# One stream of attention pairs: who empties v's product, when row sums are inverted, and who cuts the diagonal blocks

## The chip, the cores and the metric

One NeuronCore of one Trainium2 chip runs the whole program. The metric is the time of one execution in microseconds (us) on the device; lower is better. The kernel before takes 553.42 us, the median of three runs (552.69 to 554.0).

## The reference, cut to what matters

Attention over 4 batches of 8 heads with 576 positions and 64 dimensions in a head, then two layers on its output:

```
q_rot, k_rot = rotate(q), rotate(k)
scores = q_rot @ k_rot.T / sqrt(64)
scores = scores - max(scores, axis=-1)
attn = exp(scores); attn = attn / (sum(attn, axis=-1) + 1e-9)
x = (attn @ v), heads side by side                # (4, 576, 512)
h = gelu(x @ w_in); u, v = halves of h            # w_in, w_out, ... are float64
gated = u * (w_sg @ layer_norm(v) + b_sg)
x = x + gated @ w_out
out = (sigmoid(causal_conv(x)) * (x @ w_val)) @ w_out2
```

Only the attention is touched by the change. Its products must hold float32 precision: q and k are split into a high and a low part (tiles QH, QL, KH, KL), and three products of them are added.

## The kernel before, in words

The 32 heads are worked off as 16 **pairs** (pair 0 to 15), two heads on the upper and the lower 64 partitions. In `phase(i)` TensorE computes the exponents of pair i and, between them, the scores of pair i+1 that are needed only for their row maximum. The order of these units is written out by hand in `ORDERS` (line 25): a letter for the unit and a digit for the PSUM slot (`PS[0]` to `PS[3]`, two banks each). The letters are:

- `t`: one of eight units of the transposed scores of pair i (`st_unit`, line 663): three split products and the product that subtracts the row maximum, 8 matmuls. ScalarE takes the exponential out of PSUM into a tile `e` (line 674).
- `T`: the same for the last 64 keys of both heads (line 671). It reads KRH and KRL, k's last 64 columns laid out as diagonal blocks of a 128x128 tile.
- `y` and `x`: scores of pair i+1 for the maximum (`s_unit`, line 612): 2 matmuls of 320 columns or 4 of 256. VectorE reduces them with a maximum (line 615).
- `S`: the same for the last 64 queries (line 622). It reads QR, q's last 64 columns as diagonal blocks; VectorE reduces it at line 624.

Below, a unit is named by its letter and its place in the order: y0, t1, y2, t3, t4, x5, t6, t7, t8, y9, t10, t11, y12, x13, T14, S15 for pairs 1 to 14. With the digits 0123012301230120 the slot of y0 is used again by t4 (and by t8, y12 and S15), that of x5 by y9 and x13.

After the phase come the product with v (`pv_unit`, line 698, then line 708), which always accumulates in slot 3, and the row sums (`sum_unit`, lines 732 and 735) in slot 2, with 24 matmuls at line 732 in pairs 1 to 8 and 16 in pairs 9 to 14, where GpSimd adds up more of the exponentials beforehand (`FOUR = 9`). The next pair's y0 follows at once. Slot 3 is then next written by t3, slot 2 by y2. Slot 3 is emptied by two copies into the tile XU, ScalarE for one head (line 712; in the profile L264, the helper's line) and VectorE for the other (line 713). The sums go through ScalarE (line 738) and a transposing transfer into RC (line 742); `sum_end` joins the two halves and inverts them on VectorE (lines 747 and 749: 128x9 elements) and stores them (line 753).

Between the last maximum and the next y0, VectorE rotates q and k of pair i+2 (`prep_high`, line 565 and 566, L260 in the profile), ScalarE rounds them (QP, QH, KH by L264), and in pairs 1 to 8 VectorE also converts a piece of a float64 weight (`wa_half`, lines 311 to 317). At the end of `prep_high` two transfers cut KRH out of KH (line 569, issued on SyncE by line 455) and ScalarE cuts QR out of the rotated q with two 64x64 copies (lines 573 to 576).

The order inside every engine but TensorE is set by a planner, `Plan`. Each piece of work is added with an engine, a cost, and keys that it reads and writes; `after` names more pieces that must be done first. The planner lets each engine take, of what is ready by its clock, the piece with the earliest due time. TensorE keeps the order of the program:

```
        if eng == "PE":
            if self.last_pe is not None:
                deps.add(self.last_pe)
            self.last_pe = k
```

So each queue is in order on the chip, and an instruction that waits holds up what stands behind it. `sum_end(i - 1)` is called behind the phase of pair i: in pairs 1 to 8 once S15 is reduced, in pairs 9 to 14 once the low part of k is made.

Of the kernel before, what the change touches and what calls it, by code (L numbers as in the profile page):

```python
# [21 lines left out]
B, HP, S, DM, HALF = 4, 4, 576, 512, 288  # L22
NPAIR = B * HP
FOUR = 9
ORDERS = ('xtttyttytyttyxTS', '0123012301230120'), ('ytyttxtttyttyxTS', '0123012301230120'), ('ttttttttT', '012012012')
UNITS = ((0, 0), (1, 0), (0, 1), (1, 1), (2, 0), (2, 1), (3, 0), (3, 1))


# [143 lines left out]
def mixer_kernel(ctx: ExitStack, tc: tile.TileContext, qk, v, cs, w_in, g_ln, w_sgT, b_sg,  # L172
# [387 lines left out]
    def prep_high(i, after):  # L560

        j2, j3 = i % 2, i % 3
        for j in (0, 1):
            raw, kr = RAW[j2][:, j], ("raw", j2, j)
            tt("D", lambda raw=raw: raw, lambda raw=raw: raw, lambda: cst, ALU.mult, 2 * S, [("cst",)], [kr], after)
            after = [tt("D", lambda raw=raw: raw[:, 0], lambda raw=raw: raw[:, 0], lambda raw=raw: raw[:, 1], ALU.add, S, [], [kr])]
            if j:
                acopy(lambda: KH[j3], lambda raw=raw: raw[:, 0], S, [kr], [("kh", j3)])
                dma(32, lambda q: dg(q, KRH[j3], KH[j3]), [("kh", j3)], [("krh", j3)], n=2)
            else:  # L570
                acopy(lambda: QP[j2], lambda raw=raw: raw[:, 0, 0:512].rearrange("r (p c) -> r c p", c=4), 1100, [kr], [("qp", j2)])
                acopy(lambda: QH[j3], lambda raw=raw: raw[:, 0], S, [kr], [("qh", j3)])
        for h in range(2):
            rows = slice(64 * h, 64 * h + 64)
            acopy(lambda rows=rows: QR[j3][rows, rows], lambda rows=rows: RAW[j2][rows, 0, 0, 512:S], 64, [("raw", j2, 0)], [("qr", j3)],
                  P.writer["kh", j3])
        return after

    def low_part(e, i, j, after):
# [108 lines left out]
    def pv_unit(i, us):  # L688
# [21 lines left out]
        add("PE", FP32 + 0.1, mm, [("e", EU[i, 8]), ("vm", j2)], [kp])  # L710
        xu = XU[j2]
        acopy(lambda: xu[:, 0], lambda: pv[:, 0, 0:HALF], HALF, [kp], [("xu", j2, 0)])
        add("DVE", dve(HALF), lambda: nc.vector.tensor_copy(xu[:, 1], pv[:, 1, 0:HALF]), [kp], [("xu", j2, 1)])

        def st(q):
            for hf in range(2):
# [55 lines left out]
    def attention():  # L772
# [3 lines left out]
        def phase(i, vl):  # L776

            nt, xs, ys = 0, iter(range(2)), iter(range(2, 6))
            for x, (what, k) in enumerate(zip(*ORDERS[(1 if i + 1 < NPAIR else 2) if i else 0])):
                k = int(k)  # L780
                if what in "tT":
                    u = 8 if what == "T" else nt
                    st_unit(i, u, PS[k], ("ps", k))
                    add_unit(i, u)
                    nt += what == "t"
                else:
                    s_unit(i + 1, {"x": xs, "y": ys, "S": iter((8,))}[what].__next__(), PS[k], ("ps", k))
                if not x:
                    first = [P.last_pe, *vl]
                    if 2 <= i + 1 < NPAIR:  # L790
                        prep_low(i + 1, first)
                if x == (12 if i < FOUR else 0):
                    job_s(i, [P.last_pe])
            if i + 1 < NPAIR:
                s_end(i + 1)

        vl = []
        for i in range(NPAIR):
# [6 lines left out]
            phase(i, vl)  # L805
            ep.append(P.last_pe)
            rot = [P.last_pe]
            if 0 < i < FOUR or i == NPAIR - 1:
                sum_end(i - 1, [*rot, *P.writer.get(("mn", (i + 1) % 2, 1), ())] if i + 1 < NPAIR else ())
            if i + 2 < NPAIR:  # L810
                rot = prep_high(i + 2, [P.last_pe, *P.writer[("mn", (i + 1) % 2, 1)]])
            vl = job_v(i, [P.last_pe], rot)
            if FOUR <= i < NPAIR - 1:
                sum_end(i - 1, P.writer["kl", (i + 1) % 3])
            for us in ((0, 2), (1, 3), (4, 5), (6, 7)):
                pv_unit(i, us)
            sum_unit(i, PS[2], ("ps", 2))
# [417 lines left out]
```

## Time and profile before

| what | value |
|---|---|
| median of three runs | 553.42 us (552.69 to 554.0) |
| the profiled execution, its own time | 551.67 us |
| its span, first to last instruction | 549.9 us |
| granted TensorE clock, whole span | 1.00 of full speed |
| TensorE / VectorE / ScalarE / GpSimd busy | 98% / 76% / 52% / 45% |
| attention | from the start to about 235 us |

The rest of the program, from about 235 us on, is the two layers (line 835). A timeline row gives start, duration, engine, line, operation, tiles written and read, shape, count, and in brackets how long the engine was idle before it and what ended that. Matmuls overlap, so the difference of two starts tells more than a duration; a matmul row that is longer than its neighbours of the same shape has waited. The engines' busy shares are averages over stages with different limits.

### The profile page before, as it was taken

The numbers are of one execution on the slowest core, as the hardware profiler recorded it, in microseconds if no ns is written. First come the engines' busy times: TensorE is split into PE (matmuls) and PEld (weight loads), VectorE is DVE, ScalarE is ACT, GpSimd is POOL, SyncE is SP. The second block draws the span as 40 slices with busy tenths as digits, with TensorE's granted clock in tenths as the row PEclk, the third lists the DMA queues.
The fourth block names the chain that finished last, engine by engine and source line by source line (L and its number), as shares of the span: only waits on it lengthen the run. The fifth ranks groups of instructions, "written<-read, shape, count | busy, mean of one in ns | idle before, by whom it ended". The sixth has DMA issues, their size and how long they took to land.

```text
span 549.9 us, 12860 instructions
## 1 busy us (share of the span) xinstructions
PE 540.3 (98%) x5104; PEld 463.2 (84%) x5104; DVE 416.2 (76%) x627; ACT 283.4 (52%) x479; POOL 246.0 (45%) x231
## 2 busy tenths in 40 slices
PE   7999999999999999999999999999999999999996
PEld 6877777777777777679989989989999998899985
DVE  7888888888888888869478945653989997659610
ACT  3577777777766667635426236134157443333311
POOL 6545555555555555446886676653610011221000
PEclk9999999999999999999999999999999999999999
DMA  5465655565665564674384662634364112110022
GB/s 191 137 195 139 178 155 170 152 184 159 202 162 165 154 203 96 185 248 116 125 277 145 207 214 73 212 106 147 108 213 130 65 44 77 39 58 2 0 77 95
DMA packets 55404, 77.07 MB, mean 140 GB/s; under 512 B 26768, under 2 KB 31376, under 8 KB 55344
## 3 DMA queue, kind: packets, MB, share of 16 engines
q1 hardware_dynamic: 55040, 75.98, 45.2%
q8 instruction: 40, 0.66, 0.5%
q10 hardware_dynamic: 304, 0.26, 0.1%
q14 instruction: 20, 0.16, 0.1%
HBM read 55.94 MB, written 18.95 MB: 136 GB/s over the span
## 4 chain that ended last, share of the span: by engine, by line
PE 80%; DVE 11%; DMA 3%; ACT 2%; issue 2%; SPq 0%; POOL 0%; DVEq 0%; ACTq 0%; POOLq 0%
PE psa L835 52%; PE psa L663 11%; PE psa L698 7%; DVE raw L260 5%; PE psa L612 3%; DVE mx L615 3%; PE psa L732 2%; PE psa L671 2%; ACT e L674 2%; PE psa L946 2%; DMA rr<-r_d 2%; PE psa L708 1%; DMA xs<-xu_d 1%; DMA raw<-qk 1%; ACT kh L264 1%
## 5 line engine op out<-in xcount | busy, mean ns | idle before, releaser
L615 DVE TENSOR_REDUCE mx<-psa 128x2 f32<-128x640 f32 (+1 forms) x96 | 88.7, 954 | 21.6 <-PE psa L612 14.3
L674 ACT ACTIVATE e<-psa 128x576 f32<-128x576 f32 x144 | 88.4, 652 | 17.8 <-PE psa L671 9.1
L698 PE MATMUL psa<-e,vm 128*32 128x288 f32 x1024 | 65.4, 408 | 0.0
L698 PEld LDWEIGHTS psa<-e,vm 128*32 128x32 f32 x1024 | 31.6, 110 | 27.8 <-issue 2.6
L261 POOL TENSOR_TENSOR ac<-e,e 128x576 f32<-128x576 f32 x32 | 45.4, 1435 | 8.1 <-ACT e L674 8.0
L835 PE MATMUL psa<-s_h,vn 128*128 128x288 f32 x256 | 46.8, 295 | 0.0
L264 ACT CAST qp<-raw 128x512 fp32r<-128x512 f32 x16 | 19.1, 1195 | 45.7 <-DVE raw L260 39.4
L260 DVE TENSOR_TENSOR raw<-raw,cst 128x1152 f32<-128x1152 f32 (+1 forms) x33 | 42.2, 1278 | 0.2 <-DMA raw<-qk 0.2
L663 PE MATMUL psa<-qh,kh 64*128 64x288 f32 x256 | 41.9, 309 | 0.0
L663 PE MATMUL psa<-qh,kl 64*128 64x288 f32 x256 | 40.0, 296 | 0.0
L663 PE MATMUL psa<-ql,kh 64*128 64x288 f32 x256 | 39.0, 291 | 0.0
L663 PE MATMUL psa<-mr,one_r 64*128 64x288 f32 x256 | 39.0, 291 | 0.0
L835 PEld LDWEIGHTS psa<-s_h,vn 128*128 128x128 f32 x256 | 38.3, 188 | 0.0
L261 POOL TENSOR_TENSOR vs<-vs,u 128x576 f32<-128x576 f32 x16 | 26.7, 1666 | 20.5 <-DVE vs L950 20.5
L612 PE MATMUL psa<-kh,qp 64*128 64x320 f32 (+1 forms) x256 | 32.9, 313 | 1.8 <-ACT kh L264 1.7
L1027 DVE SCALAR_TENSOR_TENSOR gt<-xm,cw,gt 128x576 f32<-128x576 f32 x32 | 29.0, 910 | 1.8 <-ACT gt L1024 1.4
L612 PEld LDWEIGHTS psa<-kh,qp 64*128 64x128 f32 x256 | 21.6, 184 | 9.5 <-ACT kh L264 7.2
L663 PEld LDWEIGHTS psa<-qh,kh 64*128 64x128 f32 x256 | 25.8, 184 | 3.3 <-DVE mx L615 1.5
L835 PE MATMUL psa<-XH,w_l 128*128 128x288 f32 x128 | 27.4, 296 | 0.1
L835 PE MATMUL psa<-XL,w_h 128*128 128x288 f32 x128 | 27.3, 295 | 0.0
L835 PE MATMUL psa<-XH,w_h 128*128 128x288 f32 x128 | 27.3, 295 | 0.0
L835 PE MATMUL psa<-s_l,vn 128*128 128x288 f32 x128 | 27.3, 294 | 0.0
(185 smaller groups left out, 1474.3 us busy)
## 6 DMA issues: line engine op xcount, KB each, us to landing
raw<-qk SPq DMA_DIRECT2D x31, 576.0 KB
vm<-v SPq DMA_DIRECT2D x16, 288.0 KB
xu_d<-xu SPq DMA_DIRECT2D x32, 144.0 KB
rb<-r_d SPq DMA_DIRECT2D x32, 144.0 KB
xs<-xu_d SPq DMA_DIRECT2D x16, 288.0 KB
x_d<-xs SPq DMA_DIRECT2D x16, 288.0 KB
g_d<-vs SPq DMA_DIRECT2D x16, 288.0 KB
wr<-w_in SPq DMA_DIRECT2D x8, 512.0 KB
```

The costliest lines, as they stand in the source:

```text
L260: return add("DVE", dve(n), lambda: nc.vector.tensor_tensor(out_(), a(), b(), op), r, w, after, lock=True)
L261: return add("Pool", pool(n), lambda: nc.gpsimd.tensor_tensor(out_(), a(), b(), op), r, w, after, lock=True)
L264: return add("Act", act(n), lambda: nc.scalar.copy(out_(), in_()), r, w, after)
L612: nc.tensor.matmul(ps[:, h, w * y:w * y + w], QP[j2][rows, c], kh[rows, keys], start=True, stop=True)
L615: add("DVE", MAXIMA[n // 2 > 0][1], lambda: nc.vector.tensor_reduce(out=MX[j2][:, n // 2 > 0, :, chunks[0]:chunks[-1] + 1], in_=ps[:, :, 0 ...
L663: nc.tensor.matmul(ps[:, h, 0:HALF], x[rows, keys] if o < 3 else x[rows], y[rows, cols], start=o == 0, stop=o == 3)
L671: nc.tensor.matmul(ps[:, hf, 0:HALF], x, y[:, cols], start=o == 0, stop=o == 3)
L674: add("Act", 0.62, lambda: nc.scalar.activation(E[n], ps[:, :, 0:HALF], AF.Exp), [kps], [("e", n)])
L698: nc.tensor.matmul(pv[32 * t:32 * t + 32, h, 0:HALF], VM[j2][:, 128 * j + 64 * h + 32 * (t % 2):128 * j + 64 * h + 32 * (t % 2) + 32], E[E ...
L732: nc.tensor.matmul(ps[32 * t:32 * t + 32, 0, 0:HALF], ones[h], a[:, h], start=n == 0, stop=False, skip_group_check=True)
L835: nc.tensor.matmul(out_(y), lhs(p, k, y), rhs(q, k, y), start=not z, stop=ends and z == len(terms) - 1)
L1027: add("DVE", dve(S) + 0.05, lambda dd=dd, m=m, x2=x2, gt=gt: nc.vector.scalar_tensor_tensor(gt(), x2()[:, m:m + S], cw[:, 5 * dd + m:5 * d ...
```

## The change

Four edits, all in the attention. (1) For pairs 0 to 8 ScalarE makes both copies out of v's product; from pair 9 on VectorE keeps one. (2) `sum_end(i - 1)` is called inside the phase of pair i, behind the unit at place 8, for all pairs 1 to 15. (3) KRH is cut by two ScalarE copies behind the phase of the pair before, and QR by two transfers behind QH; before, it was the other way round. (4) Pairs 9 to 14 have an order of their own, in which the third y moves from place 12 to place 8: y0, t1, y2, t3, t4, x5, t6, t7, y8, y9, t10, t11, t12, x13, T14, S15, over the same slots.

```diff
-ORDERS = ('xtttyttytyttyxTS', '0123012301230120'), ('ytyttxtttyttyxTS', '0123012301230120'), ('ttttttttT', '012012012')
+ORDERS = ('xtttyttytyttyxTS', '0123012301230120'), ('ytyttxtttyttyxTS', '0123012301230120'), ('ttttttttT', '012012012'), ('ytyttxttyytttxTS', '0123012301230120')
...
             if j:
                 acopy(lambda: KH[j3], lambda raw=raw: raw[:, 0], S, [kr], [("kh", j3)])
-                dma(32, lambda q: dg(q, KRH[j3], KH[j3]), [("kh", j3)], [("krh", j3)], n=2)
             else:
...
                 acopy(lambda: QH[j3], lambda raw=raw: raw[:, 0], S, [kr], [("qh", j3)])
-        for h in range(2):
-            rows = slice(64 * h, 64 * h + 64)
-            acopy(lambda rows=rows: QR[j3][rows, rows], lambda rows=rows: RAW[j2][rows, 0, 0, 512:S], 64, [("raw", j2, 0)], [("qr", j3)],
-                  P.writer["kh", j3])
+                dma(32, lambda q: dg(q, QR[j3], QH[j3]), [("qh", j3)], [("qr", j3)], n=2)
...
         acopy(lambda: xu[:, 0], lambda: pv[:, 0, 0:HALF], HALF, [kp], [("xu", j2, 0)])
-        add("DVE", dve(HALF), lambda: nc.vector.tensor_copy(xu[:, 1], pv[:, 1, 0:HALF]), [kp], [("xu", j2, 1)])
+        if i < FOUR:
+            acopy(lambda: xu[:, 1], lambda: pv[:, 1, 0:HALF], HALF, [kp], [("xu", j2, 1)])
+        else:
+            add("DVE", dve(HALF), lambda: nc.vector.tensor_copy(xu[:, 1], pv[:, 1, 0:HALF]), [kp], [("xu", j2, 1)])
...
-            for x, (what, k) in enumerate(zip(*ORDERS[(1 if i + 1 < NPAIR else 2) if i else 0])):
+            for x, (what, k) in enumerate(zip(*ORDERS[0 if not i else 2 if i + 1 == NPAIR else 1 if i < FOUR else 3])):
...
+                if x == 8 and i:
+                    sum_end(i - 1, [P.last_pe])
                 if x == (12 if i < FOUR else 0):
                     job_s(i, [P.last_pe])
             if i + 1 < NPAIR:
                 s_end(i + 1)
+            if 2 <= i + 1 < NPAIR:
+                k3 = (i + 1) % 3
+                for h in range(2):
+                    rows = slice(64 * h, 64 * h + 64)
+                    acopy(lambda rows=rows: KRH[k3][rows, rows], lambda rows=rows: KH[k3].bitcast(F32)[rows, 512:S], 64, [("kh", k3)], [("krh", k3)], [P.last_pe])
...
-            if 0 < i < FOUR or i == NPAIR - 1:
-                sum_end(i - 1, [*rot, *P.writer.get(("mn", (i + 1) % 2, 1), ())] if i + 1 < NPAIR else ())
...
-            if FOUR <= i < NPAIR - 1:
-                sum_end(i - 1, P.writer["kl", (i + 1) % 3])
```

## Rows read from the trace of the kernel before

**Rows 1.** The page, busy time, share and instructions of each engine.
```profile
PE 540.3 (98%) x5104; PEld 463.2 (84%) x5104; DVE 416.2 (76%) x627; ACT 283.4 (52%) x479; POOL 246.0 (45%) x231
```
**Rows 2.** Stretches: length, busy PE, PEld, DVE, ACT, POOL, then clock and DMA.
```profile
31.77:45.34 13.57, 13.57 (x198) 10.00 (x194) 11.74 (x16) 9.80 (x19) 4.87 (x4) 1.00 0.64 191
45.34:142.89 97.55, 97.55 (x1363) 71.26 (x1359) 85.96 (x134) 69.85 (x122) 49.49 (x42) 1.00 0.55 158
142.89:222.97 80.08, 79.12 (x1120) 58.74 (x1116) 70.36 (x102) 55.56 (x101) 46.45 (x41) 1.00 0.60 165
169.86:183.52 13.66, 13.49 (x187) 9.89 (x187) 11.78 (x16) 9.01 (x17) 7.92 (x8) 1.00 0.60 165
209.99:222.97 12.98, 12.98 (x186) 9.74 (x186) 11.42 (x20) 9.69 (x19) 7.75 (x7) 1.00 0.40 95
```
**Rows 3.** Chain of waits at the end of pair 4: the row sums.
```profile
84.88 1.46 PE psa L732 x24
```
**Rows 4.** Timeline of TensorE, start of pair 5: y0, first matmuls of t3, t4.
```profile
87.16 0.41 PE L612 MATMUL psa<-kh,qp 64*128 64x320 f32 x2
...
88.08 0.52 PE L663 MATMUL psa<-qh,kh 64*128 64x288 f32 x2
...
88.94 0.40 PE L663 MATMUL psa<-qh,kh 64*128 64x288 f32 x2
```
**Rows 5.** Timeline of VectorE, start of pair 5.
```profile
87.28 0.42 DVE L317 SCALAR_TENSOR_TENSOR wf<-wr,wt 128x256 int32<-128x256 int32 x1
87.63 0.20 DVE L749 RECIPROCAL rc<-rc 128x9 f32<-128x9 f32 x1
87.75 0.40 DVE L713 COPY xu<-psa 128x288 f32<-128x288 f32 x1
88.06 1.55 DVE L615 TENSOR_REDUCE mx<-psa 128x2 f32<-128x640 f32 x2
```
**Rows 6.** Timeline of ScalarE, start of pair 5.
```profile
86.29 0.67 ACT L264 CAST kh<-raw 128x576 fp32r<-128x576 f32 x1 [0.29 <-DVE raw L260]
...
87.31 0.39 ACT L264 COPY xu<-psa 128x288 f32<-128x288 f32 x1
...
88.22 0.65 ACT L674 ACTIVATE e<-psa 128x576 f32<-128x576 f32 x1 [0.26 <-PE psa L663]
89.09 4.50 ACT L674 ACTIVATE e<-psa 128x576 f32<-128x576 f32 x7 [0.21 <-PE psa L663]
```
**Rows 7.** Timeline of ScalarE, start of pair 11: copy of v's product, QR's two copies.
```profile
170.01 0.39 ACT L264 COPY xu<-psa 128x288 f32<-128x288 f32 x1
170.29 0.50 ACT L264 CAST qr<-raw 64x64 fp32r<-64x64 f32 x2
```
**Rows 8.** Timeline of TensorE, pair 14: t8's first matmuls, y9, t10's first.
```profile
213.29 0.30 PE L663 MATMUL psa<-qh,kh 64*128 64x288 f32 x2
...
213.82 0.39 PE L612 MATMUL psa<-kh,qp 64*128 64x320 f32 x2
214.04 0.29 PE L663 MATMUL psa<-qh,kh 64*128 64x288 f32 x2
```
**Rows 9.** Timeline of VectorE, pair 14: the maxima of x5 and y9.
```profile
212.51 1.22 DVE L615 TENSOR_REDUCE mx<-psa 128x4 f32<-128x1024 f32 x1 [0.47 <-PE psa L612]
214.25 0.82 DVE L615 TENSOR_REDUCE mx<-psa 128x2 f32<-128x640 f32 x1 [0.51 <-PE psa L612]
```
**Rows 10.** Timeline of TensorE: y0 of pair 12.
```profile
183.52 0.41 PE L612 MATMUL psa<-kh,qp 64*128 64x320 f32 x2 [0.17 <-ACT kh L264]
```
**Rows 11.** Timeline of SyncE: transfers of row sums in pairs 5 and 11.
```profile
87.30 1.24 SPq L742 DMA_DIRECT2D rc<-ss  x2
...
172.79 1.23 SPq L742 DMA_DIRECT2D rc<-ss  x2
```
**Rows 12.** Timeline of ScalarE after S15 of pair 5.
```profile
98.02 1.20 ACT L264 CAST qp<-raw 128x512 fp32r<-128x512 f32 x1 [2.19 <-DVE raw L260]
```
**Rows 13.** Waits of TensorE's weight loads in the layers: total, times, longest.
```profile
PEld psa L835 <- POOL w_l L261: 0.3, 1, 0.3
```

## The prediction, before the result was known

> **What bounds the kernel now.** I read the page first. TensorE is busy 98% of the span [rows 1], but a matmul that waits for its PSUM slot counts as busy, so the share doesn't say whether it is held up. The stretches by pair do. Pair 14 takes 12.98 us [rows 2] and shows no wait inside. Pairs 1 to 8 have eight more matmuls for row sums; 24 take 1.46 us [rows 3], so eight take 0.49, and a pair of that kind without a wait should last 12.98 + 0.49 = 13.47. Pair 1 takes 13.57; pairs 2 to 8 together 97.55 [rows 2], that is 13.94 each: 97.55 - 7 x 13.47 = 3.3 us are lost in them.
>
> Where, the start of pair 5 shows. y0 starts at 87.16, t3 at 88.08, t4 at 88.94 [rows 4]: 0.86 us from t3 to t4, where one t unit takes 0.53 (t8 to y9 in pair 14, 213.29 to 213.82 [rows 8]). t3's first matmuls last 0.52 in place of 0.30. t3 writes slot 3, and VectorE's copy frees half of that only at 87.75 + 0.40 = 88.15. t4 writes y0's slot, and the maximum of y0 (0.82 for one such [rows 9]) starts behind that copy at 88.06 and ends at 88.88. VectorE was held by the weight's conversion to 87.70, the reciprocal from 87.63 and the copy from 87.75 [rows 5]. So TensorE waits here for VectorE's queue, once in a pair.
>
> In pairs 9 to 14 (80.08 us for six, 13.35 each [rows 2]) the loss is mixed: y0 of pair 12 comes 0.17 us late for the rounded k [rows 10], pair 11 (13.66) also has the stall at t4, pair 14 has nothing.
>
> **Part 1: ScalarE makes both copies, pairs 0 to 8; the reciprocal is gone from there.** Removed from VectorE at the start of pairs 2 to 9: the copy (0.40, 0.31 to the next start) and 0.20 of reciprocal. The maximum of y0 can then start when the conversion ends, 87.70, and end at 88.52. t3 runs 0.53 from 88.08, so t4 wants 88.61 and waits no more. Added on ScalarE: the second copy. The first starts at 87.31 [rows 6], what follows such a copy starts 0.28 later (170.01 to 170.29 [rows 7]), so the second runs from 87.59 to 87.98. The half of slot 3 that it frees is wanted by t3's second matmul, at 88.08 or a little later: free in time by 0.1 or more. The first exponential starts at 88.22 after 0.26 of idle time [rows 6], so ScalarE has room, the more as QR's two copies (0.50 [rows 7]) leave this place. Late next would be the rounded k that y0 reads; it is done at 86.29 + 0.67 = 86.96, 0.20 ahead of y0 [rows 4, 6], and both follow from the same last maxima, so that margin moves along. With no wait left, pairs 1 to 8 fall to 13.47; I take 13.50 because pair 1, with neither conversion nor reciprocal ahead of its copy, still showed 13.57. 13.57 + 97.55 - 8 x 13.50 = **3.1 us gained**. Bounds: nothing, if another wait takes over at once, and 13.57 + 97.55 - 8 x 13.47 = 3.4. I lean to the upper end since the row next to it, pair 1, is already there.
>
> The Trainium skill, page "PSUM — Partial Sum Buffer", section "Specifications (TRN2)", speaks against this part: ScalarE and VectorE may read PSUM side by side at full rate where they use different banks, so two engines should empty the slot sooner than one. By it the second half would be free at 87.31 + 0.39 = 87.70, and the change would make that 0.28 later, nine times, 2.5 us lost in place of 3.1 gained. The trace doesn't bear that out: VectorE came to its copy only at 87.75 [rows 5], and the sum goes by that row; the rule's case is rival (e).
>
> **Part 2: row sums in the score stretch.** Two small VectorE instructions (0.20 for the reciprocal [rows 5], the join no longer) move behind place 8. VectorE idles 0.51 us ahead of y9's maximum [rows 9], so they cost nothing if their input has landed. It is issued at 87.30 to 88.54 in pair 5, 0.14 us behind y0, but at 172.79 to 174.02 in pair 11, 2.93 us behind y0 at 169.86 [rows 2, 11]. Place 8 is reached 3.3 us behind y0 (213.29 - 209.99), so pairs 1 to 8 are safe. In pairs 9 to 14 a late landing would hold up the maxima queued behind, y9's above all, and x13 waits for the slot of y9. Cost 0, upper bound 0.5 in each of six pairs; I take 0, since VectorE will have the maxima of y8 and y9 to do first.
>
> **Part 3: diagonal blocks.** SyncE issues two transfers of the same size as before, only for q and, in ScalarE's order, ahead of k; the S15 of the phase after reads them. ScalarE's two copies move to behind S15, where it idles 2.19 us ahead of QP [rows 12]. That covers 0.50. Cost 0; without that cover 0.50 a pair (rivals).
>
> **Part 4: the new order, pairs 9 to 14.** It moves y to place 8, so y9 follows with no t between. y9 uses x5's slot. In pair 14 x5's maximum runs from 212.51 to 213.73, and VectorE had waited 0.47 for x5, so it can't start sooner [rows 9]. The order before gave y9 at 213.82, just behind it [rows 8]. Now y8 takes t8's place at 213.29 and passes on after 0.22 (y9 to t10 [rows 8]) or, by its columns, 0.15 (two matmuls of 288 columns are a quarter of a unit's 0.53, two of 320 a ninth more), so y9 wants 213.44 to 213.51 and gets 213.79 (VectorE's end plus 0.06, as t4 came 88.94 after 88.88 [rows 4, 5]). That is a **new wait** of 0.28 to 0.35, I take 0.34, and about 0.10 for the restart (t4's first matmuls last 0.40 against 0.30 [rows 4, 8]). In return the last maximum no longer queues behind y12's, but x13 and S15 come later by the same wait, so the rotation starts about when it did and the rounded k is not late for a TensorE that is itself later. I make each pair 12.98 + 0.44 = 13.42, pair 9 and 11 included, whose stall at t4 part 1 or the missing row sum removes: 6 x 13.42 - 80.08 = **0.4 us lost**. Bounds: 6 x 12.98 - 80.08 = -2.2 (no new wait, no late k) and 6 x 13.66 - 80.08 = +1.9 (each as long as pair 11 was).
>
> **Behind the attention** TensorE waits for 0.3 us only [rows 13], on a chain that starts from S15 of pair 14 and moves with it. I take 0, and ±0.5 for the planner, which lays all queues anew.
>
> **Sum.** -3.1 + 0.4 = -2.7 us against the profiled execution: 551.67 becomes 549.0, its span 549.9 becomes 547.2. That execution lies 1.75 below the median, so the median goes from 553.42 to **550.7**. A measurement of this kernel can tell about 0.2%, 1.1 us, from no change.
>
> **Rivals.** (a) *The exponentials take the gain.* ScalarE runs seven of them without a gap, 4.50 us [rows 6]. The first of these can start at best when the one ahead ends, 88.87 in place of 89.09: 0.22 sooner, not 0.4. If T14 then waits for its slot, eight pairs gain 0.22 each: -1.8 + 0.4, 552.0. For it: the gapless run. Against: pair 14 has the same run and no wait. Chance 0.20, somewhat over half of it within 0.2%.
>
> (b) *Slower: the diagonal copies fall among the exponentials.* Place: ScalarE's queue, behind the next pair's first exponential. 0.50 us in a gapless run delays T14 by up to that much in 14 pairs: 550.7 + 7.0 = 557.7, at half the price 554.2. It decides from the point where they start later than t3's exponential. Against it: they are ready right where ScalarE idles. Chance 0.08.
>
> (c) *The new order pays*: y9 doesn't wait. Then part 4 is -2.2 and the time 548.1. Against it: VectorE waited for x5. Chance 0.05.
>
> (d) *The copy wasn't what held t3 and t4*, so that the change doesn't do what it says: something else in VectorE's queue stays as late, only part 4 remains, 553.8. Against it: the four rows of VectorE that follow each other without a gap [rows 5]. Chance 0.06.
>
> (e) *ScalarE's second copy is the late one*: it runs behind its first in any case, and if VectorE would have been free at pv's end, nine starts lose 0.28 each and gain nothing: 553.4 + 2.5 + 0.4 = 556.3. Against it: 87.75. Chance 0.04.
>
> **How the numbers follow.** The forecast has 0.57: 0.54 faster, 0.03 within 0.2%. With (a) 0.09 and 0.11, (c) 0.05 faster, (d) 0.05 within and 0.01 slower, (b) 0.08 and (e) 0.04 slower: faster 0.68, same 0.19, slower 0.13. The range runs from 549.4, the forecast less the planner's 0.5, part 1's upper bound (0.3) and 0.5 for a wait at y9 that turns out shorter, to 553.4, no change, which takes in (a) and part 4 at its upper bound (552.2). It leaves out (b), (c), (e) and most of (d).
>
> **What would show it.** Pairs 2 to 8 at about 13.5; t4 0.53 behind t3; VectorE going from the conversion straight to y0's maximum. In pairs 9 to 14 y9 about 0.5 us behind y8, released by the maximum, and pairs of 13.4. The diagonal copies in ScalarE's gap behind T14. I am wrong if t4 still comes over 0.7 behind t3, if pairs 9 to 14 fall under 13.2, or if VectorE stands idle ahead of the row sums.

## The result, and the profile after

The changed kernel takes 549.84 us, the median of 15 executions (549.05 to 552.66); the kernel before, on the same chip, 553.70 (15 executions, 552.58 to 557.95). The ratio, 0.992, is that of the means (550.03 and 554.44); its 95% interval is 0.9899 to 0.9942. Applied to the 553.42 that the forecast started from, it gives a gain of about 4.4 us (3.2 to 5.6) where 2.7 were forecast, and a time of 549.0, just below the range. The medians differ by 3.9 us, and the median 549.84 by itself lies inside the range. The forecast has the right direction and too small a size. The profiled execution took 551.03 us (span 549.2). A second one, a_again below, took 549.15 (span 547.4), closer to the median.

The page of the changed kernel, busy time by engine:

```profile
PE 539.1 (98%) x5104; PEld 463.0 (84%) x5104; DVE 413.8 (75%) x618; ACT 284.7 (52%) x488; POOL 246.2 (45%) x231
```

Against [rows 1], VectorE has 9 instructions and 2.4 us less, ScalarE 9 more and 1.3 us more: the nine copies. (The diagonal copies only change tile, from QR to KRH.) The stretches that answer to [rows 2]: pair 1, pairs 2 to 8, pairs 9 to 14, pair 11, pair 14.

```profile
32.52:46.00 13.48, 13.48 (x199) 10.01 (x196) 11.39 (x15) 10.00 (x19) 4.89 (x4) 1.00 0.65 189
46.00:140.68 94.68, 94.68 (x1363) 70.24 (x1359) 83.19 (x127) 70.87 (x130) 49.52 (x42) 1.00 0.59 165
140.68:221.51 80.83, 79.59 (x1120) 58.61 (x1116) 71.30 (x103) 55.61 (x102) 46.34 (x41) 1.00 0.63 163
167.62:181.02 13.40, 13.21 (x190) 9.73 (x187) 11.83 (x16) 8.95 (x17) 7.87 (x8) 1.00 0.67 174
208.11:221.51 13.40, 13.22 (x190) 9.75 (x186) 12.00 (x21) 9.51 (x19) 7.69 (x7) 1.00 0.40 90
```

Pairs 1 to 8 take 13.48 + 94.68 = 108.16 us, 108.0 were forecast. Pairs 9 to 14 take 80.83 (80.43 in a_again), 80.52 were forecast. So the attention's two sums came out as forecast, and the rest of the gain must lie elsewhere.

The start of pair 5, TensorE, answers to [rows 4]: y0, t3's first two products, t4's first.

```profile
86.59 0.41 PE L608 MATMUL psa<-kh,qp 64*128 64x320 f32 x2
...
87.51 0.34 PE L659 MATMUL psa<-qh,kh 64*128 64x288 f32 x2
87.65 0.34 PE L659 MATMUL psa<-qh,kl 64*128 64x288 f32 x2
...
88.04 0.35 PE L659 MATMUL psa<-qh,kh 64*128 64x288 f32 x2
```

From t3 to t4 it is 0.53 us, where it was 0.86. VectorE at the same place, for [rows 5]:

```profile
86.69 0.43 DVE L317 SCALAR_TENSOR_TENSOR wf<-wr,wt 128x256 int32<-128x256 int32 x1
87.04 0.21 DVE L748 RECIPROCAL rc<-rc 128x9 f32<-128x9 f32 x1
87.16 1.50 DVE L611 TENSOR_REDUCE mx<-psa 128x2 f32<-128x640 f32 x2
```

The copy is gone and the maxima start right behind the reciprocal. But the reciprocal has not gone. Before, the join stood at the start of every even pair from 2 to 8; the planner now puts it into the score stretch in all of them but pair 2, and leaves the reciprocal at the start of each pair from 2 to 9. ScalarE, for [rows 6]: both copies in one row, then eight exponentials without a gap.

```profile
86.71 0.70 ACT L264 COPY xu<-psa 128x288 f32<-128x288 f32 x2
87.66 4.99 ACT L670 ACTIVATE e<-psa 128x576 f32<-128x576 f32 x8 [0.25 <-PE psa L659]
```

In pair 14 TensorE shows the new wait, where [rows 8] had none: y8, y9, t10.

```profile
211.46 0.31 PE L608 MATMUL psa<-kh,qp 64*128 64x320 f32 x2
211.95 0.42 PE L608 MATMUL psa<-kh,qp 64*128 64x320 f32 x2 [0.18 <-DVE mx L611]
212.20 0.30 PE L659 MATMUL psa<-qh,kh 64*128 64x288 f32 x2
```

y9 comes 0.49 us behind y8, about 0.5 was forecast, and the releaser is the maximum of x5. Last, TensorE's waits over the whole program: y9's, and those of its weight loads in the layers, which answer to [rows 13].

```profile
PE psa L608 <- DVE mx L611: 0.9, 5, 0.2
...
PEld psa L837 <- POOL w_l L261: 0.8, 1, 0.8
PEld psa L837 <- ACT w_h L264: 0.5, 1, 0.5
```

Behind the attention this execution waits longer than the one that the prediction read, not less.

**The stages.** The table splits the span of several profiled executions at the same instructions. The *junction* is the time from the end of the attention to TensorE's first product with s_h; in it TensorE multiplies the attention's output with w_in. a_again is the changed kernel again, the b_again kernels are the kernel before again.

```
                      before  b_again b_again2 b_again3  after  a_again
to the first y0         9.03     8.96     9.43     8.96   9.79     9.00
pair 0                 22.74    22.72    22.72    22.72  22.72    22.70
pairs 1 to 8          111.11   111.13   111.12   111.10 108.16   108.18
pairs 9 to 14          80.09    80.08    80.07    80.07  80.84    80.43
pair 15                12.14    12.14    12.16    12.15  12.15    12.14
junction               26.61    28.15    30.90    26.51  27.84    27.18
rest of the layers    288.16   288.03   288.02   288.02 287.73   287.74
span                  549.88   551.22   554.42   549.52 549.24   547.37
```

From pair 0 to pair 15 nothing differs between executions of one kernel by more than 0.41 us. The junction of the kernel before does: 26.5 to 30.9.

**Two kinds of execution.** By their granted clock the executions of the kernel before fall into two groups. Beside the experiments it was executed 113 times with its clock noted. In 62 the mean granted clock was 0.998 or more, and the time 551.24 to 555.47, median 553.14. In 51 it was 0.992 to 0.997, and the time 555.49 to 558.95, median 556.70. The two ranges of time adjoin, so that the time alone would not part the groups. The changed kernel had 0.998 or more in all 16 executions. The three times that the forecast started from (552.69 to 554.0) all lie in the first group by their time; of the 15 beside the changed kernel, five lie in the second.

So the gain has two terms. From the first group to the changed kernel: 553.14 - 549.84 = 3.3 us, of which the attention gives 2.6 (a_again: 2.93 in pairs 1 to 8, less 0.35 in pairs 9 to 14) and the layers 0.3. And 51 in 113 executions of the kernel before stand 3.6 us higher, 1.6 us in the mean; that term the forecast did not have. Together that would be 4.9; the means of the 15 and 15 executions, with five of the 15 in the second group, differ by 4.4.

### The profile page after: what moved, and what is told of

It reads as the page before. It is cut to its first block, busy times and chain, and to the rows that moved or that the text cites. A ratio compares the mean times of both kernels' runs of the same rounds, so it can differ in the third digit from the quotient of the medians.

```text
span 549.2 us, 12869 instructions
## 1 busy us (share of the span) xinstructions
PE 539.1 (98%) x5104; PEld 463.0 (84%) x5104; DVE 413.8 (75%) x618; ACT 284.7 (52%) x488; POOL 246.2 (45%) x231
## 4 chain that ended last, share of the span: by engine, by line
PE 88%; DVE 4%; DMA 2%; ACT 2%; POOL 1%; issue 1%; SPq 1%; DVEq 0%; ACTq 0%; POOLq 0%
PE psa L837 52%; PE psa L659 10%; PE psa L694 10%; PE psa L608 4%; PE psa L731 3%; PE psa L667 3%; DVE mx L611 2%; PE psa L704 2%; PE psa L948 2%; PE psa L761 1%; DVE raw L260 1%; ACT e L670 1%; DMA wr<-w_in 1%; PE psa L618 1%; DMA rc<-ss 1%
## 5 line engine op out<-in xcount | busy, mean ns | idle before, releaser
L670 ACT ACTIVATE e<-psa 128x576 f32<-128x576 f32 x144 | 87.2, 651 | 21.2 <-PE psa L659 9.4
L659 PE MATMUL psa<-qh,kh 64*128 64x288 f32 x256 | 40.4, 300 | 0.0
L608 PE MATMUL psa<-kh,qp 64*128 64x320 f32 (+1 forms) x256 | 35.0, 317 | 2.0 <-DVE mx L611 0.9
```

Of the source, the lines that this page charges most:

```text
L608: nc.tensor.matmul(ps[:, h, w * y:w * y + w], QP[j2][rows, c], kh[rows, keys], start=True, stop=True)
L659: nc.tensor.matmul(ps[:, h, 0:HALF], x[rows, keys] if o < 3 else x[rows], y[rows, cols], start=o == 0, stop=o == 3)
L670: add("Act", 0.62, lambda: nc.scalar.activation(E[n], ps[:, :, 0:HALF], AF.Exp), [kps], [("e", n)])
```

## What makes the second group

The trace of b_again2 (556.21 us, clock 0.995) shows it. TensorE in the junction, in the middle of the products with w_in:

```profile
251.39 0.43 PE L835 MATMUL psa<-XH,w_l 128*128 128x288 f32 x2
253.75 0.54 PE L835 MATMUL psa<-XH,w_h 128*128 128x288 f32 x2 [1.93 <-ACT w_h L264]
254.12 0.43 PE L835 MATMUL psa<-XL,w_h 128*128 128x288 f32 x2
255.10 0.69 PE L835 MATMUL psa<-XH,w_l 128*128 128x288 f32 x2 [0.55 <-POOL w_l L261]
255.58 0.68 PE L835 MATMUL psa<-XH,w_h 128*128 128x288 f32 x2
...
258.46 0.55 PE L835 MATMUL psa<-XH,w_h 128*128 128x288 f32 x2
258.85 0.43 PE L835 MATMUL psa<-XL,w_h 128*128 128x288 f32 x2
```

It waits 1.93 us for the high part of the last of eight pieces of w_in and 0.55 for the low part; then two matmuls last 0.68 in place of 0.43 for a while. The windows of that stretch (the last three numbers are the granted clock, the DMA share and GB/s):

```profile
255.31:258.72 3.41, 3.41 (x16) 3.41 (x16) 3.09 (x7) 2.11 (x4) 3.08 (x5) 0.50 0.33 77
```

The clock is 0.50 there, the lower level of 1.2 GHz, for 3.41 us: 1.7 us lost, besides 2.5 us of waiting; 30.90 - 26.5 is 4.4. The Trainium skill, page "TensorE: Matmul & The Clock Gate", section "Part 1: The HAM clock gate", says that an idle TensorE falls to half its clock; this trace agrees in so far as the clock fell behind these two waits.

The piece is late because of what stands ahead of it. In b_again2 the piece lands, ScalarE takes its absolute value, VectorE converts it from float64, ScalarE makes w_h of it. ScalarE, and below it the last step of VectorE's conversion:

```profile
248.61 0.66 ACT L321 ACTIVATE wt<-wr 128x512 f32<-128x512 f32 x1 [6.91 <-DMA wr<-w_in]
249.96 1.28 ACT L902 ACT_TABLE_LOAD   x1 [0.69 <-DVE wt L313]
251.25 1.94 ACT L902 ACTIVATE gl<-psa 128x1024 f32<-128x1024 f32 x2
253.07 0.62 ACT L264 CAST w_h<-wf 128x512 fp32r<-128x512 f32 x1
```

```profile
251.93 0.43 DVE L317 SCALAR_TENSOR_TENSOR wf<-wr,wt 128x256 int32<-128x256 int32 x1
```

VectorE is done at 252.36, and the cast starts at 253.07 behind a table load and the first GELUs in ScalarE's queue. So the late landing makes most of the wait, and ScalarE's queue the last 0.7 us of it.

The same in the execution that the prediction read, ScalarE and then TensorE:

```profile
249.96 0.61 ACT L264 CAST w_h<-wf 128x512 fp32r<-128x512 f32 x1
```

```profile
251.24 0.42 PE L835 MATMUL psa<-XH,w_h 128*128 128x288 f32 x2
```

There w_h is ready at 250.57 and wanted at 251.24: no wait, but only 0.67 us of room, at the end of a chain of transfers on SyncE's queue (lines 742, 717, 842, 324). In the four traces of the kernel before, w_h is ready 14.5, 15.5, 16.8 and 18.2 us behind the end of the attention, and TensorE wants it about 16.1 us behind it. In the two traces of the changed kernel it is ready after 16.5 and 15.8 us: the room is no larger there, and these traces don't show why the long wait is rarer. Pieces 7 and 8 share one raw buffer, so the load of piece 8 comes behind the conversion of piece 7 too.

## The experiments

Names beginning with a_ are the changed kernel with something put back or added, those with b_ the kernel before with one edit. "Low" counts executions with a mean granted clock of 0.997 or less.

**The changed kernel and the kernel before again.**

> The changed kernel once more, for a second profile. Theory A: pairs 1 to 8 again about 108.2 us, pairs 9 to 14 about 80.8; the first y0 up to 1 us earlier than 9.8 us after the start, and less waiting between attention and layers than the 1.1 us that the first profile has over the kernel before. Theory B: pairs 1 to 14 differ by over 1 us from 189.0.

> The kernel before once more, for a second profile of it. Timed runs put the change at a ratio of 0.992, some 4.4 us, while the two profiles differ by 0.7 us in span: the attention is 2.2 us shorter, the start 0.8 us longer and the stretch between attention and layers 1.1 us longer in the changed one. Theory A (start and junction are luck of the transfers): here the attention up to pair 15 takes what it took in the first profile (pairs 1 to 8 within 0.3 us of 111.1, pairs 9 to 14 within 0.5 of 80.1), and start or junction differ by 1 us or more. Theory B (the attention of the kernel before is usually slower than in its one profile): pairs 1 to 14 together take 193 us or more in place of 191.2.

a_again took 549.15, b_again 553.03; the stages are in the table above. b_again2 and b_again3, profiled later on another chip, took 556.21 and 551.31.

> The kernel before a third time, to get a profile of an execution with a mean granted clock under 0.998, some half of its runs. If it is one: all of the 4 to 5 us that such a run takes more lies in one stretch of about 9 us at half of the clock. Theory A puts that stretch between attention and layers, after a wait of TensorE for weights; theory B puts it inside the attention.

> The kernel before a fourth time, for the same reason and with the same expectations as the third. If it is an execution at full clock: pairs 1 to 8 again 111.1, pairs 9 to 14 80.1, the first y0 within 1 us of 9.0, and the stretch behind the attention between 26.6 and 28.2.

**The old order back (a_oldorder), and another one (a_y10).**

```diff
-            for x, (what, k) in enumerate(zip(*ORDERS[0 if not i else 2 if i + 1 == NPAIR else 1 if i < FOUR else 3])):
+            for x, (what, k) in enumerate(zip(*ORDERS[(1 if i + 1 < NPAIR else 2) if i else 0])):
```

> The changed kernel with the order of before in pairs 9 to 14. If y9's wait is the price of the new order: no wait at y9, but y0 of each of these pairs waits some 0.2 us for the rounded k as in the kernel before, so 13.2 us each, about 79.2 together, 1.6 us less than the change. If the new order pays as a whole, this is slower than the change, 82 us or more for the six.

a_oldorder: 549.83 us (548.81 to 554.05, 9 executions, 2 low). Pairs 9 to 14 take 80.45 against 80.43: four of them take 13.3 and pair 14 takes 12.96, but pair 9 takes 14.33. So the new order neither gains nor loses within the attention of the changed kernel. Why pair 9 is long there is not shown; at the length of its neighbours the old order would be some 1.0 us shorter.

a_y10 moves the third y of pairs 9 to 14 to place 10, with a t between:

```diff
-('ytyttxttyytttxTS', '0123012301230120')
+('ytyttxtttyyttxTS', '0123012301230120')
```

> The changed kernel with the third y of pairs 9 to 14 at place 10 in place of 8, so that t8 stands between x5 and y9 again. If the wait of y9 for the maximum of x5 is what lengthens these pairs, they fall from 13.47 us to between 13.0 and 13.1 each, 80.8 to about 78.5 together, 2.3 us less than the change. If those pairs are held by the rounded k instead, they stay at 13.3 or more and nothing is gained.

a_y10: 549.24 us (548.02 to 553.98, 6 executions, 1 low), ratio to before 0.9896 (0.9844 to 0.9948). Pairs 9 to 14 take 79.78, that is 13.3 each, and not the 13.0 to 13.1 expected: y9's wait is gone, but T14's weight load then waits 0.2 us for y10's maximum in its slot. That is 0.65 us less in the attention than in a_again; the times, 549.24 and 549.84, with their spread don't tell the two kernels apart.

**The copies alone (b_copy), and the change without them (a_dvecopy).**

```diff
-        add("DVE", dve(HALF), lambda: nc.vector.tensor_copy(xu[:, 1], pv[:, 1, 0:HALF]), [kp], [("xu", j2, 1)])
+        if i < FOUR:
+            acopy(lambda: xu[:, 1], lambda: pv[:, 1, 0:HALF], HALF, [kp], [("xu", j2, 1)])
+        else:
+            add("DVE", dve(HALF), lambda: nc.vector.tensor_copy(xu[:, 1], pv[:, 1, 0:HALF]), [kp], [("xu", j2, 1)])
```

> The kernel before with the first edit alone: ScalarE makes both copies for pairs 0 to 8; row sums, diagonal blocks and order as before. In the changed kernel the reciprocal still stands at the start of every pair, against what the prediction assumed, and the stall at t4 is gone all the same. If the copy alone was the cause, pairs 1 to 8 fall from 111.1 to 108.2 to 108.8 us here (t4 within 0.1 us of its place), pairs 9 to 14 keep 80.1 but for pair 9 (13.3 to 13.4 in place of 13.65). If the join or the diagonal copies on ScalarE hold t3 or t4 as well, pairs 1 to 8 stay above 109.5. The executions with a mean granted clock of 0.992 to 0.997, 14 of 29 of the kernel before against 3 of 32 with the change in it: if the stalls at t4 bring them, there are 2 or fewer of 5 or more here.

> The change without its first edit: VectorE makes the second copy again in all pairs. If the copy is the cause of the stall at t4, pairs 1 to 8 return to 110.5 to 111.5 us, and pairs 9 to 14 take 80.4 to 81.2. If the moved join is worth something of its own, pairs 1 to 8 come to 109.5 or less. If the low-clock executions hang on the stalls, they are about half of the runs here; if they hang on the new order or the transfers of QR, they are rare.

b_copy: 551.69 us (549.90 to 554.81, 12 executions, 6 low), ratio 0.9947 (0.9915 to 0.9979). a_dvecopy: 553.01 (552.02 to 554.02, 12, none low), ratio 0.9966 (0.9945 to 0.9988). Without the copies pairs 1 to 8 stay at 111.50, so rival (d) is out: the copy was what held t3 and t4. But the copies alone give less than the whole. The windows of pairs 1 to 8 in b_copy:

```profile
31.95:141.31 109.36, 109.36 (x1558) 80.84 (x1554) 94.78 (x142) 80.19 (x149) 54.44 (x46) 1.00 0.58 169
```

That is 1.75 of the 2.95 us. Odd pairs take 13.48, even ones 13.8 to 13.9. What the even pairs still wait for, the next two runs tell. Pairs 9 to 14 take 79.71 there, 0.4 us less than before, where the changed kernel with its new order takes 0.35 to 0.75 more. The six executions of b_copy that are not low have a median of 550.35, so at full clock the copies alone give about 2.8 of the 3.3 us. And b_copy, 1.75 us shorter in its attention, had as many low executions as the kernel before: its trace, of a low execution, waits 3.0 us for w_h and its junction takes 32.10.

**The change without the row sums (a_oldsums) and without the diagonal blocks (a_olddiag); each alone (b_sums, b_diag).** The edits are the hunks of the change taken back, or made alone: for the row sums

```diff
-                if x == 8 and i:
-                    sum_end(i - 1, [P.last_pe])
...
+            if 0 < i < FOUR or i == NPAIR - 1:
+                sum_end(i - 1, [*rot, *P.writer.get(("mn", (i + 1) % 2, 1), ())] if i + 1 < NPAIR else ())
...
+            if FOUR <= i < NPAIR - 1:
+                sum_end(i - 1, P.writer["kl", (i + 1) % 3])
```

and for the diagonal blocks

```diff
+                dma(32, lambda q: dg(q, KRH[j3], KH[j3]), [("kh", j3)], [("krh", j3)], n=2)
...
-                dma(32, lambda q: dg(q, QR[j3], QH[j3]), [("qh", j3)], [("qr", j3)], n=2)
...
+            acopy(lambda rows=rows: QR[j3][rows, rows], lambda rows=rows: RAW[j2][rows, 0, 0, 512:S], 64, [("raw", j2, 0)], [("qr", j3)],
+                  P.writer["kh", j3])
...
-                    acopy(lambda rows=rows: KRH[k3][rows, rows], lambda rows=rows: KH[k3].bitcast(F32)[rows, 512:S], 64, [("kh", k3)], [("krh", k3)], [P.last_pe])
```

> The changed kernel with the row sums (join, reciprocal and their transfers) back at their two old places. Theory S (the extra gain of about 1.7 us beyond the attention comes from the row sums: in the old place the last two pairs' rc, xu_d and r_d transfers stand in another order in SyncE's queue, the last piece of w_in lands later, TensorE waits 2 to 3 us for it in some executions and runs at half clock behind that): the junction from the attention to the first s_h product is 28 us or more in many executions, about half of the executions show a granted clock of 0.997 or lower; median 550.5 to 552. Theory D (the extra gain comes from the diagonal blocks): the junction stays at 27 to 28, at most 1 execution in 12 shows a lower clock, median 549.5 to 550.5. In both, pairs 1 to 8 rise from 108.2 to about 109.4, since the join and the reciprocal are back at the start of the even pairs (before with the copies alone: 109.36), and pairs 9 to 14 stay at 80.4.

> The changed kernel with the diagonal blocks as before (k's by transfer, q's by ScalarE). Theory S: nothing to be seen, 549.2 to 550.3, at most 1 execution in 12 at a granted clock of 0.997 or lower, junction 27 to 28 us, pairs 1 to 8 at 108.2. Theory D: about half of the executions at the lower clock, junction 28 us or more in those, median 550.5 to 552.

> The kernel before with the row sums alone in the score stretch. Theory S: executions at a granted clock of 0.997 or lower all but vanish (at most 1 in 12, against about 4 in 10 of the kernel before), median 552 to 553; pairs 1 to 8 stay near 111.1 to 111.5 because the second copy still holds VectorE. Theory D: as the kernel before, about half of the executions at the lower clock, median 553.5 to 556.

> The kernel before with the diagonal blocks alone as in the change. Theory S: as the kernel before, about half of the executions at a granted clock of 0.997 or lower, median 553.5 to 556. Theory D: lower-clock executions all but vanish, median 552 to 553. In both, pairs 1 to 8 at 111.1 and pairs 9 to 14 at 80.1: the diagonal copies cost nothing within the attention.

Pairs 1 to 8 went the other way round than expected: a_oldsums 108.56, a_olddiag 109.35. Their windows:

```profile
32.60:141.16 108.56, 108.56 (x1556) 80.37 (x1552) 94.81 (x142) 81.17 (x148) 54.40 (x46) 1.00 0.59 167
```

```profile
32.38:141.73 109.35, 109.35 (x1557) 80.83 (x1554) 94.80 (x142) 80.12 (x148) 54.35 (x46) 1.00 0.60 169
```

So with the copies on ScalarE, taking back the diagonal blocks costs 109.35 - 108.16 = 1.2 us and taking back the row sums 0.4 (0.25 in a_oldsums2 below). The two are not apart: in a_olddiag the planner also put the join back at the start of pairs 4, 6 and 8. Against a_oldsums and a_oldsums2, which have the join there too, the diagonal blocks are worth 0.8 to 0.9. The start of pair 6 in a_olddiag shows why, ScalarE first (y0 starts at 100.61):

```profile
100.38 0.40 ACT L741 ACTIVATE ss<-psa 128x288 f32<-128x288 f32 x1
100.80 0.24 ACT L264 CAST qr<-raw 64x64 fp32r<-64x64 f32 x1
101.07 0.70 ACT L264 COPY xu<-psa 128x288 f32<-128x288 f32 x2
```

and TensorE, t3's first two products:

```profile
101.53 0.68 PE L663 MATMUL psa<-qh,kh 64*128 64x288 f32 x2
101.83 0.52 PE L663 MATMUL psa<-qh,kl 64*128 64x288 f32 x2
```

One QR copy stands between the row sums and the copies out of slot 3, so the copies end at 101.77, behind t3's first products, and the second comes 0.30 behind the first in place of 0.14. In a_oldsums it is VectorE that is late. Pair 8 there (y0 starts at 127.50), and then in the changed kernel (y0 starts at 127.20):

```profile
127.90 0.17 DVE L746 TENSOR_REDUCE rc<-rc 128x9 f32<-128x18 f32 x1
128.10 0.21 DVE L748 RECIPROCAL rc<-rc 128x9 f32<-128x9 f32 x1
128.23 1.50 DVE L611 TENSOR_REDUCE mx<-psa 128x2 f32<-128x640 f32 x2
```

```profile
127.58 0.21 DVE L748 RECIPROCAL rc<-rc 128x9 f32<-128x9 f32 x1
127.70 1.53 DVE L611 TENSOR_REDUCE mx<-psa 128x2 f32<-128x640 f32 x2
```

The join puts y0's maximum at 0.73 us behind y0, against 0.50, and t4 pays for part of the difference: it comes 0.62 behind t3, against 0.53. Pairs 4 and 8 are 0.14 to 0.19 longer by it; pairs 2 and 6 hardly differ.

In the kernel before, each of the two alone gives nothing there: b_sums 111.17, b_diag 111.53 against 111.11. The copies have to go first. In pairs 9 to 14 b_diag takes 81.16 and not the 80.1 expected; pair 12 lasts 14.57.

The times: a_oldsums 549.88 (548.94 to 550.02, 6 executions), a_olddiag 550.30 (550.19 to 551.69, 6), none low in either; b_sums 553.26 (551.78 to 554.48, 12, none low), ratio 0.9979 (0.9957 to 1.0002); b_diag 554.10 (551.95 to 558.09, 12, 5 low), ratio 0.9997 (0.9968 to 1.0026). From the b_ side theory S (the row sums make the second group) holds, and b_sums gains nothing beyond that: its median is that of the first group, 553.14. From the a_ side theory S does not hold, since a_oldsums had no low execution. a_oldsums2 below asks again.

**The last piece of w_in, later and earlier.** a_late delays its load in the changed kernel, b_wr and a_wr give it a raw buffer of its own:

```diff
-    wa_load(7, ())
+    wa_load(7, P.writer["r_d", 15])
```

```diff
     def place(n):
-        return n % 2 if n < 6 else 0
+        return n % 2
...
-            wa_load(6, P.writer["xs", 1])
+            for n in (6, 7):
+                wa_load(n, P.writer["xs", 1])
```

(with the conversion of both pieces moved ahead of the point where the attention's buffers are given back).

> The changed kernel with the last w_in piece loaded only behind the last row sums' transfer to r_d, so about 2 to 3 us later. Theory W (TensorE's wait for the piece brings the half clock): a wait of 2 to 4 us ahead of the last product with w_h, and behind it a stretch of some 3 us at half clock in most executions (granted clock 0.997 or lower in over half), median 552 to 554. Rival (the lower clock has nothing to do with that wait): the wait alone, 551 to 552.5, clock 0.998 to 1.0 throughout.

> The kernel before with the last w_in piece in a second raw buffer, row sums untouched. Theory W: the row sums' order doesn't matter once the piece comes early: executions at a granted clock of 0.997 or lower fall to at most 1 in 12, median 551.8 to 553. Rival (the lower clock comes from the row sums in another way than by that piece): 4 in 10 as before, median 553.5 to 555.

> The changed kernel with the last w_in piece in a second raw buffer, so that its load doesn't wait for the conversion of the piece ahead. Theory W: TensorE waits no more for w_h or w_l of that piece, no execution at a lower clock, median 548.7 to 549.6 (0.2 to 0.6 less than the changed kernel). Rival: the buffers of the attention, held longer, delay the first GELU and the layers' tiles: the wait moves there, 549.8 or more.

a_late: 557.83 us (556.79 to 558.66), low in all 12 executions. TensorE in its junction, and the window behind the wait:

```profile
249.21 0.43 PE L837 MATMUL psa<-XH,w_l 128*128 128x288 f32 x2
255.31 0.85 PE L837 MATMUL psa<-XH,w_h 128*128 128x288 f32 x2 [5.67 <-ACT w_h L264]
...
257.31 0.68 PE L837 MATMUL psa<-XH,w_h 128*128 128x288 f32 x2
```

```profile
254.82:261.65 6.83, 6.32 (x25) 5.97 (x26) 3.49 (x6) 4.21 (x8) 6.32 (x6) 0.50 0.24 79
```

The delay made the wait longer than meant, 5.67 us, and the stretch at half clock twice as long. b_wr: 551.93 us (551.12 to 552.85), low in none of 12, against 15 of 35 of the kernel before on the same chip; ratio 0.9956 (0.9928 to 0.9984). Its attention is that of the kernel before, and w_h is ready at 246.57, some 5 us before TensorE comes to it:

```profile
245.95 0.62 ACT L264 CAST w_h<-wf 128x512 fp32r<-128x512 f32 x1 [3.64 <-DVE wf L317]
```

Later in the one kernel, earlier in the other, and the low executions come and go with it: that the wait for w_h of this piece makes the second group is shown. (Over all traces: behind waits of 1.93, 2.43, 3.00 and 5.67 us for w_h the clock fell, behind 0.62 and less it did not.) b_wr does not part the two things that make w_h late, since it brings the load forward and also puts the cast ahead of the GELUs in ScalarE's queue.

a_wr lost: 554.85 us (551.99 to 557.18), 9 of 12 low, as its rival said. The piece is early there too, but what the first GELU waits for has moved. ScalarE, then TensorE:

```profile
249.29 1.28 ACT L905 ACT_TABLE_LOAD   x1 [2.87 <-DMA r_d<-rc]
```

```profile
251.66 0.53 PE L838 MATMUL psa<-XH,w_h 128*128 128x288 f32 x2 [1.49 <-ACT gl L905]
```

The GELU writes where buffers of the attention lay, and its ScalarE queue waits for the last store of row sums out of them; TensorE then waits for the GELU to empty a PSUM slot. Behind this wait the clock does not fall. It falls from 268.36 on, for 3.41 us, behind a second wait, in the layers, for a tile that GpSimd writes:

```profile
267.09 0.40 PE L949 MATMUL psa<-s_h,t 128*128 128x288 f32 x1 [2.39 <-POOL t L261]
```

```profile
268.36:271.77 3.41, 3.41 (x16) 3.41 (x15) 1.75 (x2) 0.95 (x2) 3.33 (x3) 0.50 0.71 204
```

The junction takes 28.30 us, and the rest of the layers 291.98. So in a_wr the low clock of the profiled execution doesn't come from w_h, and the version that I had hoped would beat the changed kernel does not.

**Which edit makes the piece early enough.** b_tail moves only the row sums of pairs 13 and 14; b_order makes the new order alone; a_oldsums2 repeats a_oldsums for the count.

```diff
+                if x == 8 and i >= NPAIR - 2:
+                    sum_end(i - 1, [P.last_pe])
...
-            if 0 < i < FOUR or i == NPAIR - 1:
+            if 0 < i < FOUR:
...
-            if FOUR <= i < NPAIR - 1:
+            if FOUR <= i < NPAIR - 2:
```

> The kernel before with the row sums of the last two pairs but one (13 and 14) alone joined and inverted behind place 8; all else as before. Theory S-tail (the order in SyncE's queue behind the attention decides: r_d of pair 13 ahead of xu_d and w_in before, rr ahead of the last w_in piece after): executions at a granted clock of 0.997 or lower fall from about 4 in 10 to at most 1 in 12, median 552 to 553.5, pairs 1 to 8 at 111.1 and 9 to 14 at 80.1 as before. Rival (it takes the row sums of all pairs, or chance): 4 in 10 as before, median 553.5 to 555.

> The kernel before with the new order of pairs 9 to 14 alone. Pairs 9 to 14: 80.3 to 80.8 as in the changed kernel (y9 waits for the maximum of x5), pairs 1 to 8 at 111.1. If the order is among what makes the half-clock executions rare (theory O): at most 1 in 12 at a granted clock of 0.997 or lower, median 552.5 to 553.5. If it is the row sums alone (theory S): 4 or more in 12, median 553.5 to 556.

> The changed kernel with the old row sums once more, for the count alone. Theory S (the row sums alone make the half-clock executions rare): 3 or more in 12 at 0.997 or lower. Theory O (another edit, or a few together, do it as well): at most 1 in 12, median 549.3 to 550.3. Pairs 1 to 8 at 108.56 as before.

b_tail: 553.79 us (552.03 to 558.34), 4 of 12 low, ratio 0.9984 (0.9952 to 1.0016). Behind the attention SyncE issues its transfers there in the order of the changed kernel, and it did not help, so theory S-tail falls. b_order: 552.56 (552.01 to 553.68), none of 12 low against 7 of 18 of the kernel before beside it, ratio 0.9972 (0.9949 to 0.9996), although its pairs 9 to 14 are longer by 0.66 us:

```profile
142.95:223.70 80.75, 79.65 (x1120) 58.53 (x1116) 71.41 (x103) 55.52 (x101) 46.34 (x41) 1.00 0.59 165
```

a_oldsums2: 549.34 (548.82 to 550.14), none of 7 low, pairs 1 to 8 at 108.42. So theory O holds. All counts together:

```
one edit alone:       copies 6 of 12   diagonal blocks 5 of 12   row sums 0 of 12   order 0 of 12
all but one:          copies 0 of 12   diagonal blocks 0 of 6    row sums 0 of 13   order 2 of 9
none: 51 of 113       all: 0 of 16
```

Alone on the kernel before, the row sums of all pairs or the order leave no low execution; the copies or the diagonal blocks leave about half. But a_oldorder, which has the row sums and not the order, had 2 low of 9, and a_y10, with another order, 1 of 6: so it is not shown that the row sums suffice beside the other edits. Nor is it settled what the two have in common on the way to that piece: b_order keeps SyncE's order of the kernel before behind the attention, b_tail has the changed one, and the counts are the other way round.

## Why the forecast was too small, point by point

- **What bounds the kernel now** held for the attention. Pairs 1 to 8 fell from 111.11 to 108.16 us, and t4 comes 0.53 behind t3.
- **Part 1** was right in its sum (2.95 us, 3.1 forecast, bounds 0 to 3.4) and wrong in whose it is. It put the whole gain down to the copies; alone they give 1.75. The sum came out since the working took for granted that QR's copies leave their place, and the gain of that was counted here; that it came within 0.2 us is in part luck.
- **Part 2** failed in its statement that the reciprocal leaves the start of the pair: only the join did, in pairs 4, 6 and 8. Priced at 0, the row sums were worth 0.25 to 0.4 us in pairs 1 to 8 (a_oldsums2, a_oldsums).
- **Part 3**, priced at 0, was worth 0.8 to 1.2 us there once the copies stand on ScalarE (a_olddiag, the lower figure without the join that came back with it). I had looked for where the copies go and not at what they delayed where they were. On the side feared in rival (b) nothing happened: the exponentials run without a gap.
- **Part 4** was right: pairs 11 and 14 take 13.40 us (13.42 forecast), the maximum of x5 releases y9, six pairs 80.43 to 80.84 (80.52). But its comparison was with pairs that waited in other ways; in the changed kernel the old order costs the same (a_oldorder).
- **"Behind the attention ... I take 0, and ±0.5 for the planner"** is the step that failed. It stood on one row, a wait of 0.3 us for w_l [rows 13], of an execution that lay 1.75 us under the median. For w_h of the same piece there was only 0.67 us of room, behind a chain whose end moves by 3.7 us over four traces. In 51 of 113 executions the clock says that the room was not there; their median is 3.6 us higher, and the one such execution that was profiled (b_again2) lost 2.5 us to the two waits and about 1.7 to the half clock. The changed kernel rarely comes there; the counts show that its edits make this so, but by which way is open. Against the group at full clock alone, -2.7 was forecast and -3.3 measured, of which 2.9 are found in the attention and in the rest of the layers.
- **The sum** went against the median of three executions which all, by chance, lie in the full-clock group.
- **The rivals.** (a), exponentials that take the gain, didn't come: eight run without a gap, and the pairs still take 13.5. (c) is out by y9's wait, (d) by a_dvecopy, (e) by t3's second product, 0.14 behind its first; the rule of the Trainium skill, page "PSUM — Partial Sum Buffer", section "Specifications (TRN2)", that (e) goes by was of no consequence, as VectorE came to its copy only 0.44 us behind ScalarE [rows 5, 6]. That a later stage varies between executions, and that the change alters how often its long form occurs, was no rival and should have been one.

The 0.3 us in the rest of the layers, and about 0.4 us between the stages, are not explained.

## What to carry to other kernels

A wait of nothing at the end of a chain of transfers is not yet a margin: subtract when the operand was ready from when it was wanted, and compare that with how much the chain varies; several executions' times and clocks, where they fall into groups, tell of a stage that the one profiled execution doesn't show. Small copies of 0.24 us cost 0.8 to 1.2 us over eight pairs because one of them stood ahead of the instruction that frees a PSUM slot, so price a moved instruction at its old place as well as at its new one. And edits that unblock the same instruction aren't additive: row sums and diagonal blocks were worth nothing until the copies had moved.

## What the runs showed of the hardware that was not expected

TensorE's granted clock fell to 0.50 for 3.41 us after waits of 1.93 and 0.55 us for w_h and w_l (b_again2), and for 6.83 us, from just before the end of a wait of 5.67 us, in a_late. In a_wr it fell for 3.41 us behind a wait of 2.39 us in the layers, and not behind one of 1.49 us. Pairs of matmuls with w_in, which start 0.27 us apart at full clock, start 0.48 apart at half clock (255.58 to 256.06 in b_again2). Waits of 2.5 us so cost about 4.2.
